# Two attention layers on one core: the second layer's loads issued one by one, ScalarE's exponentials over two or three PSUM banks, and new scheduler weights

## The chip, the cores and the metric

The kernel runs on one core of one Trainium2 chip. The metric is device time in microseconds (us) of one launch; lower is better. Each version was run several times, and a profile was taken of one execution. Engines are named as in the profile: PE (TensorE, matrix multiplications), PEld (its weight loads), DVE (VectorE), ACT (ScalarE), POOL (GpSimd), SP (SyncE, which here only issues DMAs; SPq is its DMA queue). "L757" is line 757 of the kernel's file; the changed kernel has other line numbers for the same code.

## The reference

Two independent layers, A and B, each with 2048 tokens, 512 features and 32 heads of 16 features. A is ordinary softmax attention. B is linear attention with a softmax feature map. The outputs are put side by side.

```python
# A:  q, k, v = split(x @ wqkv)
scores = einsum("bhqd,bhkd->bhqk", q, k) * Dh ** -0.5
o = einsum("bhqk,bhkd->bhqd", softmax(scores), v)          # then  o @ wo
# B:  q, k, v = split(x @ wqkv)
pq, pk = einsum("bhsd,hdf->bhsf", q, w_phi), einsum("bhsd,hdf->bhsf", k, w_phi)
phi_q = concatenate([softmax(pq), softmax(-pq)]);  phi_k = likewise from pk
kv, z = einsum("bhsf,bhsd->bhfd", phi_k, v), sum_s(phi_k)
o = (phi_q @ kv) / (phi_q @ z + 1e-6)                      # then  o @ wo
return concatenate([a, b], axis=-1)
```

A needs 32 x 2048 x 2048, that is 134 million, exponentials. They are what the kernel is about.

## The kernel before

**A program that schedules itself.** The kernel is a Python program. Each piece of work is a `_Task` with an engine, an *assumed* duration `dur`, an assumed latency `lat` until its result can be used, and its dependencies. A greedy list scheduler (`_Sched`) keeps a clock of its own and takes, again and again, the candidate whose start time plus a small priority weight is lowest. It emits the instructions in that order. Each engine's program is that list in that order (below, VectorE waits 11.53 us at one instruction and runs none of those behind it): what the scheduler assumed wrongly can turn into waiting.

```python
sp_q = SC.stream("sp", 0.0)        # DMAs of finished units
sp_b = SC.stream("sp", 0.01)       # B's loads
pe_qd = SC.stream("pe", lambda t: -0.05 if SC.mode == "r" else 0.25)   # weights set by hand
...
c = min(cand, key=lambda c: c[1])  # c[1] = start + weight of its stream
```

**The exponentials.** A's work comes in 32 units (8 groups of four heads x 4 blocks of 512 queries) with 16 key tiles each. One key tile needs four score matmuls (four heads), each filling one PSUM bank of 128 x 512 float32. For about three quarters of the key tiles ScalarE computes the exponentials, two banks per instruction. For the others VectorE makes an approximation by integer arithmetic: four conversions of one bank and three shifted copies. PE then multiplies with V ("PV").

```python
def act_kt(u, kt):
    for half in range(2):
        qk = qk_task(u, kt, half, [("A", A_bank, 1, 1)], lambda t, i: 2 * t.res["A"].idx + i)
        ...
        return e.activation(pT[:, t.res["p"].idx, :], PS[:, b:b + 2, :].rearrange("p a n -> p (a n)"),
                            ACT.Exp, scale=0.25)
        exps.append(put(ac_ex, _Task("act", 0.92, ...)))
```

**The end of a unit.** VectorE copies the finished PSUM bank to `X`, SyncE sends the sums to `sums` by DMA, VectorE takes the reciprocal, SyncE sends it to DRAM (`scr`) and back, spread over the partitions (`Yd`), and GpSimd multiplies. `sums`, `scr` and `Yd` all go through SyncE's queue.

**B's loads** go through the same queue, each list as one task that cannot be split, at an assumed 0.5 us per DMA:

```python
def b_load(name, fn, n, deps, lat, us=0.5):
    d = dsem(name)
    return put(sp_b, _Task("sp", us * n, dma(d, lambda e, t, i: fn(e, i), n), deps, lat=lat))
...
b_wt = b_load("wt", lambda e, i: e.dma_start_transpose(w[...], B_wqkv[...]), 8, freed, 18.0)
b_x  = b_load("xb", lambda e, i: e.dma_start_transpose(xT[:, i, :], B_x[...]), 4, freed, 25.0)
```

Of the kernel before, what the change touches and what calls it, by code (L numbers as in the profile page):

```python
# [124 lines left out]
class _Task:  # L125
    __slots__ = ("eng", "dur", "lat", "deps", "emit", "need", "tok", "end", "res", "then", "rel", "done", "pre",
                 "mode", "rows", "port", "prep", "area", "gate")
# [24 lines left out]
class _Sched:  # L152
# [12 lines left out]
    def __init__(self):  # L165
        self.free = {}
        self.busy = {}
        self.streams = {}
        self.end = 0.0
        self.mode = None  # L170
        self.rows = [0.0] * 4
        self.port = {"dve": 0.0, "pool": 0.0}
        self.urgent = None
        self.last_port = None
        self.filler = None
        self.active = collections.deque()
        self.nfill = 0
        self.nforce = 0
# [8 lines left out]
    @staticmethod  # L187
    def _ready(t):
        r = 0.0
        for d in t.deps:  # L190
            if not d.done:
                return None
            if d.end > r:
                r = d.end
        for _, slots, n, _ in t.need:
            if n == 2:
                fr = [max(x.free, y.free) for x, y in zip(slots, slots[1:]) if x.left == 0 and y.left == 0]
            else:
                fr = [x.free for x in slots if x.left == 0]
            if not fr:  # L200
                return None
            r = max(r, min(fr))
        return r
# [13 lines left out]
    def _choose(self, eng, ss):  # L217
# [17 lines left out]
        if eng == "pe" and self.urgent is not None:  # L235
            u = [c for c in cand if c[2] is self.urgent]
            if u:
                due = max(u[0][3], self.free["act"] - self.MM - self.PE_LAT)
                for c in cand:
                    t = c[2]["q"][0]  # L240
                    if t.mode != "r" and c[0] + t.dur + self.SWITCH > due + 0.02:
                        c[1] += 0.4
# [48 lines left out]
    def _place(self, t, start):  # L291
# [5 lines left out]
        for key, slots, n, nrel in t.need:  # L297
            if n == 2:
                _, _, i = min((max(slots[i].free, slots[i + 1].free) > start, -i, i) for i in range(len(slots) - 1)
                              if slots[i].left == 0 and slots[i + 1].left == 0)  # L300
                got = slots[i:i + 2]
            else:
                got = sorted((x for x in slots if x.left == 0), key=lambda x: (x.free > start, x.idx))[:1]
            for x in got:
                toks += x.take(nrel)
            t.res[key] = got if n > 1 else got[0]
# [29 lines left out]

_LOG2E = 1.4426950408889634
# [6 lines left out]
def _main_path(nc, es, P, dsem, flag, A_x, A_wqkv, A_wo, B_x, B_wqkv, B_w_phi, B_wo, out):  # L344
# [4 lines left out]
    NPT = 7  # L349
    NB, NJ = 2, 4  # L350
    B_AT = (0.24, 0.54, 0.95)
# [53 lines left out]
    pT = sb("pT", [128, NPT, 1024], BF)  # L405
# [9 lines left out]
    A_bank = [_Slot(0), _Slot(1)]  # L415
    G = [_Slot(4), _Slot(5), _Slot(6), _Slot(7)]
# [15 lines left out]
    pe_qa = SC.stream("pe", -0.02)  # L432
    SC.urgent = pe_qa
    pe_tp = SC.stream("pe", -0.15)
    pe_qd = SC.stream("pe", lambda t: -0.05 if SC.mode == "r" else 0.25)
    pe_pj = SC.stream("pe", -0.03)
    pe_pa = SC.stream("pe", left_in(pt_sl, 2, 0.1))
    pe_pd = SC.stream("pe", left_in(rj_sl, 1, 0.1))
    pe_b = SC.stream("pe", 0.02)
    pe_op = SC.stream("pe", -0.03)  # L440
    one_bank = [pe_tp, pe_pj, pe_b, pe_op, pe_pa, pe_pd]
    ac_ev = SC.stream("act", -0.1)
    ac_xe = SC.stream("act", -0.2)
    ac_ex = SC.stream("act", 0.0)
    dv_x = SC.stream("dve", -0.4)
    dv_xe = SC.stream("dve", -0.3)
    dv_ev = SC.stream("dve", -0.2)
    dv_op = SC.stream("dve", -0.2)
    dv_n = SC.stream("dve", -0.15)
    dv_a = SC.stream("dve", -0.1)  # L450
    dv_ad = SC.stream("dve", 0.0)
# [3 lines left out]
    dv_ek = SC.stream("dve", -0.1)  # L455
# [160 lines left out]
    for g in range(1, 4):  # L616
        for c in range(4):
            at.append((32 * (g - 1) + 8 + 4 * c, lambda g=g, c=c: proj("k", g, c)))
        at.append((32 * (g - 1) + 10, lambda g=g: proj("q", g, 0)))
    for i in range(12):  # L620
        at.append((22 + 5 * i, lambda i=i: proj("q", i % 4, 1 + i // 4)))
# [12 lines left out]
    state = {"ua": 0, "ud": 0, "n": 0}  # L634
# [9 lines left out]

    def qk_task(u, kt, half, need, bank):
        g, c = units[u]

        def mm(e, t, i):
            return kq(e, PS[:, bank(t, i), :], u, kt, 2 * half + i)
        return _Task("pe", MM, pe_group(2, mm), [q_ready[(g // 2, c)], k_ready[(g, kt // 4)]], lat=PL, need=need,  # L650
                     mode="r", rows=(2 * half, 2 * half + 1), area=0.5)
# [50 lines left out]
    def make_unit_end(u):  # L702
# [5 lines left out]
        def after_x(_):  # L708
# [15 lines left out]
            for hf in range(2):  # L724
                cs = slice(256 * hf, 256 * hf + 256)
                ms.append(put(po_n, _Task("pool", 0.65, one("pool", lambda e, t, cs=cs: e.tensor_tensor(  # L726
# [20 lines left out]

    def act_kt(u, kt):
        exps = []
        for half in range(2):  # L750
            qk = qk_task(u, kt, half, [("A", A_bank, 1, 1)], lambda t, i: 2 * t.res["A"].idx + i)
            qk_all[u].append(qk)
            put(pe_qa, qk)

            def ex_emit(e, t, qk=qk):
                b = 2 * qk.res["A"].idx
                return e.activation(pT[:, t.res["p"].idx, :], PS[:, b:b + 2, :].rearrange("p a n -> p (a n)"),  # L757
                                    ACT.Exp, scale=0.25)
            exps.append(put(ac_ex, _Task("act", 0.92, one("act", ex_emit), [qk], lat=AL,
                                         need=[("p", pt_sl, 1, 1)], rel=[lambda qk=qk: [qk.res["A"]]])))  # L760
        put(pe_pa, pv_task(u, exps + [v_ready[kt]],
                           lambda h: VP[:, kt, v0(h):v0(h) + 32],
                           lambda r: pT[:, exps[r // 2].res["p"].idx, 512 * (r % 2):512 * (r % 2) + 512],
                           [lambda: [exps[0].res["p"], exps[1].res["p"]]]))
        close(u)

    def dve_kt(u, kt):
        npv[u] += _NPH - 1
        g, c = units[u]
# [35 lines left out]
        for j in range(1, _NPH):  # L805
            ad = put(dv_ad, _Task("dve", 0.59, one("dve", lambda e, t, j=j: e.tensor_scalar(  # L806
                rg[:, t.res["j"].idx, :], rg[:, q0.res["i"].idx, :], float(sh[j]), 32767.0, ALU.add, ALU.min)),
                firsts, lat=DL, need=[("j", rj_sl, 1, 1)], rel=[lambda: [q0.res["i"]]], port=True))
            put(pe_pd, pv_task(u, [ad, vj_ready[(kt, j)]],
# [4 lines left out]
    def src_a(_):  # L814
        while state["ua"] < NU:
            u = state["ua"]
            if a_rem[u]:
                act_kt(u, a_rem[u].pop(0))
                return
            if d_rem[u]:  # L820
                act_kt(u, d_rem[u].pop(0))
                return
            state["ua"] += 1

    def src_d(_):
        u = max(state["ud"], state["ua"])
        while u < NU and (not d_rem[u] or (u == state["ua"] and len(a_rem[u]) + len(d_rem[u]) < 4)):
# [3 lines left out]
        if u > state["ua"] and len(a_rem[u - 1]) + len(d_rem[u - 1]) > 3:  # L831
# [54 lines left out]
    pe_kf, pe_v, pe_kv, pe_qf, pe_y, pe_t, pe_o = (SC.stream("pe", x) for x in (-0.03,) * 7)  # L886
    dv_f, dv_red, dv_v, dv_kv, dv_y, dv_d, dv_ob = (SC.stream("dve", x) for x in (-0.2, -0.1, -0.12, -0.12, -0.12, -0.12, -0.15))
    dv_mn = SC.stream("dve", 0.05)
    ac_kf, ac_qf, ac_ot = (SC.stream("act", x) for x in (-0.1,) * 3)
# [5 lines left out]
    def b_load(name, fn, n, deps, lat, us=0.5):  # L895
        d = dsem(name)
        return put(sp_b, _Task("sp", us * n, dma(d, lambda e, t, i: fn(e, i), n), deps, lat=lat))

    def start_b():
# [4 lines left out]
            B_wqkv[:, (i // 4) * 512 + (i % 4) * 128:(i // 4) * 512 + (i % 4 + 1) * 128]), 8, freed, 18.0)  # L904
        b_x = b_load("xb", lambda e, i: e.dma_start_transpose(  # L905
            xT[:, i, :], B_x[0][:, i * 128:(i + 1) * 128]), 4, freed, 25.0)
# [5 lines left out]
            mask8[:].unsqueeze(1).unsqueeze(3).broadcast_to([128, 4, 8, 16]), ALU.mult)), [b_bd], pre=[t_m8], lat=GL))  # L912
# [3 lines left out]
        def fold(x, ct):  # L916
            f = put(pe_b, _Task("pe", 0.24, pe_group(4, lambda e, t, i: e.matmul(
                PS[:, t.res["b"].idx, i * 128:(i + 1) * 128], w[:, i, x * 512 + ct * 128:x * 512 + (ct + 1) * 128],
                BD[:, i, :], start=True, stop=True)), [b_wt, bd], lat=PL, need=[("b", G, 1, 1)]))
# [11 lines left out]
        def k_step(st):  # L931
# [3 lines left out]
                [b_x] + wf[1], [("b", G, 1, 2), ("e", ek_sl, 1, 2)])  # L935
# [9 lines left out]
            for a in range(2):  # L945
                ph.append(put(po_phi, _Task("pool", 1.0, one("pool", lambda e, t, a=a: e.tensor_tensor(  # L946
# [10 lines left out]
                [b_x, b_wv, bs["vb1"]], [("b", G, 1, 1), ("v", vb_sl, 1, 1)])  # L957
# [35 lines left out]
        def qf_step(cq, t4):  # L993
# [3 lines left out]
                [b_x] + wf[0], [("b", G, 1, 2), ("e", et_sl, 1, 8)])  # L997
            for a in range(2):
                ets[(cq, 2 * t4 + a)] = f, put(ac_qf, _Task("act", 0.49, one("act", lambda e, t, a=a: e.activation(  # L999
                    eT_b[f.res["e"].idx][:, a, :], bank_of(f), ACT.Exp, scale=1.0 - 2.0 * a)),  # L1000
                    [f2] + bs["kend"], lat=AL, rel=[lambda: [f.res["b"]]]))

        def q_step(st):
# [32 lines left out]
            ad = [put(po_y, _Task("pool", 0.65, one("pool", lambda e, t, k=k: e.tensor_tensor(  # L1036
# [8 lines left out]
            for k in range(2):  # L1045
                om.append(put(po_y, _Task("pool", 0.65, one("pool", lambda e, t, k=k: e.tensor_tensor(  # L1046
# [13 lines left out]
                [te, b_wo], [("b", G, 1, 1)])  # L1060
# [40 lines left out]
    c5 = P.op("pe", lambda e: e.matmul(PS[0:1, 4, 0:1], good[:], ones_t[:, 0:1], start=True, stop=True),  # L1101
              [c4] + G[0].toks)
    P.op("dve", lambda e: e.tensor_scalar(flag[0:1, 0:1], PS[0:1, 4, 0:1], 127.5, None, ALU.is_lt), [c5])
# [990 lines left out]
```

## Time and profile before

The time before the change is 829.57 us (median of four runs, 824.21 to 833.1). The profiled span is 829.5 us.

| | before |
|---|---|
| ScalarE busy | 751.4 us (91%) |
| PE busy / VectorE busy | 759.9 us / 736.3 us |
| exponentials on ScalarE | 758, two banks each (1516 banks) |
| mean granted PE clock | 0.959 |

All three large engines are about 90% busy, so shares alone don't tell what bounds the kernel. The page's chain of waits that ended last (share of the span by engine, then by engine and line) does:

```profile
ACT 59%; PE 24%; DVE 11%; SPq 3%; issue 1%; DMA 1%; POOL 0%; ACTq 0%; POOLq 0%
ACT pT L757 55%; PE PS L642 8%; PE PS L657 7%; DVE rg L795 6%; DVE rg L806 3%; PE PS L570 3%; ACT e_k L936 2%; PE PS L567 1%; ACT eT L999 1%; SPq L905 1%; SPq L902 1%; PE PS L1058 1%; PE PS L684 1%; ACT e_k L1055 1%; PE PS L525 1%
```

ScalarE's exponentials (L757) are the backbone, but two fifths of the chain lie elsewhere. The groups view (line, engine, operation, out<-in, count; then busy us, mean ns of one; then idle before it and who ended it) says the same from ScalarE's side:

```profile
L757 ACT ACTIVATE pT<-PS 128x1024 bf16<-128x1024 f32 x758 | 708.6, 1079 | 32.8 <-PE PS L642 28.2
```

**How to count ScalarE's need.** Consecutive instructions overlap, so the mean of 1079 ns is not what one costs. What counts is the distance from one end to the next when nothing is missing. In the trace this is 0.490 us for one bank, 0.917 us for two. Below, *work* is the sum of these distances over all ScalarE operations, and *loss* is the rest of the span. Before: work 743.0 us, loss 86.5 us. Where the loss lies:

| stretch (before) | loss, us |
|---|---|
| 0 to 60 us | 19.7 |
| 60 to 178 us | 6.5 |
| 178 to 232 us | 21.7 |
| 232 us to the last exponential (791.5 us) | 5.0 |
| after the last exponential (less its own work) | 33.6 |

The windows view (stretch, its length, then busy us and count of PE, PEld, DVE, ACT, POOL; then granted PE clock, DMA share, GB/s) shows the first three of these stretches:

```profile
0.00:60.00 60.00, 56.28 (x386) 19.38 (x392) 36.55 (x61) 43.64 (x53) 21.53 (x46) 1.00 0.31 72
60.00:178.00 118.00, 114.69 (x1014) 33.15 (x1028) 110.88 (x190) 110.74 (x120) 13.96 (x20) 0.99 0.05 10
178.00:232.00 54.00, 42.59 (x351) 11.83 (x348) 35.22 (x59) 36.12 (x38) 4.21 (x5) 0.72 0.38 83
```

In the third, every engine slows down at once, and the PE clock falls to 0.72 of full on average. Four timelines (start, length, then the group; in brackets the idle time before it and what ended it) tell why. First SyncE's queue:

```profile
177.36 10.71 SPq L902 DMA_TRANSPOSE w<-in_B_wqkv_dram  x8
188.12 2.48 SPq L733 DMA_DIRECT2D OT<-Oo  x4
190.64 9.43 SPq L905 DMA_TRANSPOSE xT<-in_B_x_dram  x4
200.53 0.41 SPq L907 DMA_DIRECT2D w<-in_B_wqkv_dram  x1
200.99 0.48 SPq L909 DMA_DIRECT2D woB<-in_B_wo_dram  x1
201.53 0.62 SPq L710 DMA_DIRECT2D sums<-X  x1
```

VectorE at the same time:

```profile
190.81 0.68 DVE L704 COPY X<-PS 128x512 f32<-128x512 f32 x1
...
193.81 0.68 DVE L806 TENSOR_SCALAR rg<-rg 128x2048 uint16<-128x2048 uint16 x1
206.02 0.25 DVE L713 RECIPROCAL rin<-sums 128x16 f32<-128x16 f32 x1 [11.53 <-DMA sums<-X]
```

PE, whose next matmul needs what VectorE makes after that reciprocal:

```profile
206.88 0.62 PE L657 MATMUL PS<-rg,VJ 128*32 128x512 f16 x4 [10.74 <-DVE rg L806]
```

And ScalarE:

```profile
178.48 18.51 ACT L757 ACTIVATE pT<-PS 128x1024 bf16<-128x1024 f32 x20 [2.29 <-PE PS L642]
208.07 2.96 ACT L757 ACTIVATE pT<-PS 128x1024 bf16<-128x1024 f32 x3 [11.08 <-PE PS L642]
211.64 1.02 ACT L757 ACTIVATE pT<-PS 128x1024 bf16<-128x1024 f32 x1 [0.60 <-PE PS L642]
213.16 1.02 ACT L757 ACTIVATE pT<-PS 128x1024 bf16<-128x1024 f32 x1 [0.50 <-PE PS L642]
```

`X` is complete at 191.5 us, but its sums leave only at 201.53, after all four transposing loads of B's x. VectorE's reciprocal stands next in order, so VectorE waits 11.53 us; PE waits for VectorE, ScalarE for PE. From about 199 to 230 us PE has half its clock, and ScalarE gets one pair of banks per 1.5 us instead of per 0.92 us. The windows view of that stretch (0.50 is the clock):

```profile
199.00:230.00 31.00, 23.12 (x156) 6.35 (x156) 17.35 (x28) 15.66 (x16) 2.41 (x3) 0.50 0.23 58
```

The scheduler did not see this coming: it assumed 8 x 0.5 = 4 us and 4 x 0.5 = 2 us for lists that took 10.71 and 9.43 us.

### The profile page before, as it was taken

The page shows a single profiled execution, that of the slowest core. Times are in us where ns is not written, and L with a number is a line of the kernel's source. Part 1 is how long each engine was busy: PE and PEld are TensorE (multiplying, and loading weights), DVE is VectorE, ACT ScalarE, POOL GpSimd, SP SyncE. Part 2 cuts the span into 40 slices and gives each one's busy share as a digit, 9 for nine tenths or more (in the row PEclk, how much of TensorE's full clock was granted, in tenths as well). Part 3 has the DMA queues.
Part 4 walks back from the last instruction along what each step waited for, and adds up shares of the span by engine and source line. Part 5 has one row for each costly group of instructions (what it writes and reads, how often), then busy time and mean ns, then how long its engine had stood idle before and what let it go on. Part 6 is the DMA issues. An engine that isn't in the chain of part 4 may idle for free.

```text
span 829.5 us, 17394 instructions
## 1 busy us (share of the span) xinstructions
PE 759.9 (92%) x7165; PEld 231.7 (28%) x7249; DVE 736.3 (89%) x1306; ACT 751.4 (91%) x856; POOL 157.3 (19%) x233
## 2 busy tenths in 40 slices
PE   8999999994999998999989999999999999999963
PEld 3332222221222222222222222223332222332231
DVE  2699999884698999989999999999989999999973
ACT  6879999884699999999999999999999999999930
POOL 5211011110112012221121021005222102302051
PEclk9999999997599999999999999999999999999976
DMA  7100000027000000000000000000000010001001
GB/s 150 54 8 9 11 5 8 8 48 168 7 9 10 14 19 15 12 8 11 10 4 9 27 18 9 12 8 18 15 8 18 14 22 17 20 26 31 9 23 51
DMA packets 44154, 19.61 MB, mean 24 GB/s; under 512 B 33312, under 2 KB 42016, under 8 KB 44064
## 3 DMA queue, kind: packets, MB, share of 16 engines
q1 hardware_dynamic: 42480, 17.60, 8.8%
q8 instruction: 59, 0.97, 0.5%
q10 hardware_dynamic: 1584, 0.79, 0.4%
q14 instruction: 31, 0.25, 0.1%
HBM read 7.88 MB, written 4.46 MB: 15 GB/s over the span
## 4 chain that ended last, share of the span: by engine, by line
ACT 59%; PE 24%; DVE 11%; SPq 3%; issue 1%; DMA 1%; POOL 0%; ACTq 0%; POOLq 0%
ACT pT L757 55%; PE PS L642 8%; PE PS L657 7%; DVE rg L795 6%; DVE rg L806 3%; PE PS L570 3%; ACT e_k L936 2%; PE PS L567 1%; ACT eT L999 1%; SPq L905 1%; SPq L902 1%; PE PS L1058 1%; PE PS L684 1%; ACT e_k L1055 1%; PE PS L525 1%
## 5 line engine op out<-in xcount | busy, mean ns | idle before, releaser
L757 ACT ACTIVATE pT<-PS 128x1024 bf16<-128x1024 f32 x758 | 708.6, 1079 | 32.8 <-PE PS L642 28.2
L642 PE MATMUL PS<-QT,KT 32*128 32x512 bf16 x2048 | 352.0, 389 | 21.7 <-ACT pT L757 13.1
L795 DVE TENSOR_SCALAR rg<-PS 128x512 uint16<-128x512 f32 x532 | 340.5, 680 | 18.1 <-PE PS L642 16.1
L806 DVE TENSOR_SCALAR rg<-rg 128x2048 uint16<-128x2048 uint16 x399 | 260.6, 693 | 4.6 <-PE PS L657 4.1
L642 PEld LDWEIGHTS PS<-QT,KT 32*128 32x128 bf16 x2048 | 89.5, 91 | 302.4 <-ACT pT L757 218.0
L657 PE MATMUL PS<-rg,VJ 128*32 128x512 f16 x1596 | 147.9, 389 | 11.0 <-DVE rg L806 10.7
L657 PE MATMUL PS<-pT,VP 128*32 128x512 bf16 x1516 | 151.7, 397 | 2.2 <-ACT pT L757 1.1
L657 PEld LDWEIGHTS PS<-pT,VP 128*32 128x32 bf16 x1516 | 38.3, 94 | 87.4 <-issue 65.8
L726 POOL TENSOR_TENSOR OT<-X,Yd 128x256 bf16<-128x256 f32 x32 | 22.7, 727 | 198.4 <-DVE rg L806 155.3
L946 POOL TENSOR_TENSOR w<-e_k,stat 128x512 bf16<-128x512 bf16 x32 | 33.2, 1056 | 136.1 <-DVE rmin L952 42.6
L657 PEld LDWEIGHTS PS<-rg,VJ 128*32 128x32 bf16 x1596 | 39.0, 95 | 68.4 <-issue 31.5
L657 PE MATMUL PS<-rg,VP 128*32 128x512 f16 x532 | 53.2, 390 | 0.0
L726 POOL TENSOR_TENSOR Oo<-X,Yd 128x256 bf16<-128x256 f32 x32 | 23.1, 738 | 108.1 <-DMA Yd<-scr 55.2
L1036 POOL TENSOR_TENSOR w<-w 128x272 f32<-128x272 f32 x32 | 23.8, 760 | 98.5 <-DVE w L1022 80.3
L570 PE MATMUL PS<-xT,w 128*128 128x512 bf16 x111 | 30.6, 383 | 3.5 <-issue 1.9
L1055 ACT ACTIVATE e_k<-PS 128x512 bf16<-128x512 bf16 x16 | 10.1, 631 | 20.8 <-PE PS L1052 20.8
L684 PE MATMUL PS<-ones_t,zer 128*32 128x512 bf16 x276 | 28.4, 409 | 0.0
L704 DVE COPY X<-PS 128x512 f32<-128x512 f32 x32 | 22.0, 686 | 4.8 <-PE PS L657 3.6
L1022 DVE TENSOR_TENSOR w<-PS,stat 128x408 f32<-128x408 f32 (+1 forms) x48 | 25.2, 526 | 0.6
L1046 POOL TENSOR_TENSOR w<-w,den 128x256 bf16<-128x256 f32 x32 | 19.8, 636 | 31.3 <-DVE rg L806 9.3
L1058 PE MATMUL PS<-woB,e_k 128*128 128x512 bf16 x50 | 17.5, 435 | 4.6 <-issue 1.8
L939 DVE TENSOR_REDUCE stat<-e_k 128x64 f32<-128x1024 bf16 x16 | 19.3, 1209 | 0.1
(85 smaller groups left out, 422.8 us busy)
## 6 DMA issues: line engine op xcount, KB each, us to landing
Yd<-scr SPq DMA_DIRECT2D x128, 32.0 KB, 1.8
out_dram<-OA SPq DMA_DIRECT2D x16, 128.0 KB, 1.7
out_dram<-e_k SPq DMA_DIRECT2D x16, 128.0 KB, 1.7
OT<-Oo SPq DMA_DIRECT2D x64, 16.0 KB, 1.8
w<-in_A_wqkv_dram SPq DMA_DIRECT2D x2, 384.0 KB, 4.9
OT<-in_A_x_dram SPq DMA_DIRECT2D x1, 512.0 KB, 4.6
w<-in_A_wqkv_dram ACTq DMA_DIRECT2D x1, 512.0 KB, 7.7
WOp<-in_A_wo_dram SPq DMA_DIRECT2D x1, 512.0 KB, 6.8
```

The costliest lines, as they stand in the source:

```text
L570: return e.matmul(bank_of(t), w[:, ct, c0:c0 + 128], xT[:, ct, c * 512:(c + 1) * 512], start=(ct == 0), stop=(ct == 3))
L642: return e.matmul(out_ap, KT[32 * r:32 * r + n, g, kt * 128:(kt + 1) * 128], QT[32 * r:32 * r + n, c, g // 2, :], start=True, stop=True, t ...
L657: return e.matmul(PS[32 * r:32 * r + 32, pvb[u].idx, :], lhs(8 * (g // 2) + 2 * r + g % 2), rhs(r), start=t.res["first"], stop=t.res["last ...
L684: P.op("pe", lambda e, r=r: e.matmul(PS[32 * r:32 * r + 32, pvb[u].idx, :], zer[:], ones_t[:].unsqueeze(1).broadcast_to([128, 4, 128]), st ...
L726: ms.append(put(po_n, _Task("pool", 0.65, one("pool", lambda e, t, cs=cs: e.tensor_tensor(OT[:, c % 2, g // 2, cs] if even else Oo[:, ms[0 ...
L757: return e.activation(pT[:, t.res["p"].idx, :], PS[:, b:b + 2, :].rearrange("p a n -> p (a n)"), ACT.Exp, scale=0.25)
L795: return e.tensor_scalar(rg[:, q0.res["i"].idx, 512 * r:512 * r + 512], PS[:, qk.res["D"].idx, :], ya, yb, ALU.mult, ALU.add)
L806: ad = put(dv_ad, _Task("dve", 0.59, one("dve", lambda e, t, j=j: e.tensor_scalar(rg[:, t.res["j"].idx, :], rg[:, q0.res["i"].idx, :], flo ...
L946: ph.append(put(po_phi, _Task("pool", 1.0, one("pool", lambda e, t, a=a: e.tensor_tensor(pk[ph[0].res["k"].idx][:, 512 * a:512 * a + 512]. ...
L1022: muls.append(put(dv_y, _Task("dve", 0.485, one("dve", lambda e, t, yv=yv, lo=lo, n=n: e.tensor_tensor(ysv[r0.res["y"].idx][:, 136 * lo:13 ...
L1036: ad = [put(po_y, _Task("pool", 0.65, one("pool", lambda e, t, k=k: e.tensor_tensor(y3(0)[:, 2 * k:2 * k + 2], y3(0)[:, 2 * k:2 * k + 2], ...
L1058: o1, o2 = two_step(pe_o, lambda e, t, i: e.matmul(bank_of(t), oT_b[tp.res["t"].idx][:, i, :], woB[:, i, :], start=(i == 0), stop=(i == 3) ...
```

## The change

Its intent is to stop B's loads from blocking the finished units' DMAs, and to let ScalarE take three banks at once where a bank beside the pair is free. The scheduler's priority weights were also drawn anew (all now in one table `_W`), and the buffer of exponentials holds 15 single banks instead of 7 pairs. The core of the diff, with cuts marked:

```diff
     def b_load(name, fn, n, deps, lat, us=0.5):
         d = dsem(name)
-        return put(sp_b, _Task("sp", us * n, dma(d, lambda e, t, i: fn(e, i), n), deps, lat=lat))
+        return [put(sp_b, _Task("sp", us, dma(d, lambda e, t, r, i=i: fn(e, i)), deps, lat=lat)) for i in range(n)]
 ...
-            B_wqkv[...]), 8, freed, 18.0)
+            B_wqkv[...]), 8, freed, 4.0, 1.32)
-            xT[:, i, :], B_x[0][:, i * 128:(i + 1) * 128]), 4, freed, 25.0)
+            xT[:, i, :], B_x[0][:, i * 128:(i + 1) * 128]), 4, freed, 8.0, 2.5)
 ...   # PSUM: pairs at banks 0-1 and 3-4, single bank 2 beside both
-    A_bank = [_Slot(0), _Slot(1)]
-    G = [_Slot(4), _Slot(5), _Slot(6), _Slot(7)]
+    A_bank = [_Slot(0), _Slot(3)]
+    G = [_Slot(5), _Slot(6), _Slot(7), _Slot(2)]
 ...   # score matmuls are now taken from a list `pend`, two or three at a time
+            if len(pend) > 2 and x.left == 0 and x.free <= max(own.free, SC.free["pe"]) + 0.02 and \
+                    sum(y.left == 0 for y in G) > _W["el"]:
+                n = 3
 ...
+        us = 0.187 + 0.3657 * n            # the assumed duration of an exponential over n banks
+            return e.activation(pT[:, p:p + n, :].rearrange("p a n -> p (a n)"),
+                                PS[:, b:b + n, :].rearrange("p a n -> p (a n)"), ACT.Exp, scale=0.25)
 ...   # the guard that keeps long PE work from delaying score matmuls
-                due = max(u[0][3], self.free["act"] - self.MM - self.PE_LAT)
+                due = max(u[0][3], self.free["act"] + self.ahead() - self.MM - self.PE_LAT - _W["early"])
-                        c[1] += 0.4
+                        c[1] += _W["guard"]        # 0.346
 ...   # all weights and positions, e.g.
-    pe_tp = SC.stream("pe", -0.15)
-    pe_qd = SC.stream("pe", lambda t: -0.05 if SC.mode == "r" else 0.25)
+    pe_tp = SC.stream("pe", _W["tp"])                                              # -0.276
+    pe_qd = SC.stream("pe", lambda t: _W["qd_r"] if SC.mode == "r" else _W["qd_o"])  # 0.115, 0.235
-    B_AT = (0.24, 0.54, 0.95)          # when B's phases start
+    B_AT = (_W["b0"], _W["b1"], _W["b2"])                                          # 0.315, 0.54, 0.99
```

## The prediction

> **What bounds the kernel now.** The chain of waits that ended last is 59% ScalarE, 55% of it the exponentials over two PSUM banks. The groups view gives 758 of them, 1079 ns each; in the chain they follow each other every 0.917 us (22 in 20.18 us). Single-bank ScalarE operations follow every 0.49 us (two in 0.98). So ScalarE needs about 758 x 0.917 + some 97 smaller operations = 742 us; the other 85-88 us of the 829.5 us span are time in which it starved. By windows (length minus operations times cadence):
> - 0-60 us: 20 us lost (loads, projections);
> - 120-178: 7.6 us;
> - 197-232: 18.5 us;
> - 232-791: about 3 us in all, ScalarE is saturated;
> - after 791: 35 us, the serial tail.
>
> The loss at 197-232 is one event. The timeline of the SyncE queue shows 8 transposing loads of B's weights (10.7 us), 4 copies, then 4 transposing loads of B's x (9.4 us), each list one indivisible step. The sums of a finished unit, whose X copy ended at 191.4 us, are sent only at 201.5 us; VectorE's reciprocal waits 11.5 us for them and holds up everything behind it in order. ScalarE idles 197-208, and PE's granted clock then is 0.5 until about 230 us, when ScalarE gets one pair per 1.5 us. The Trainium skill ("TensorE: Matmul & The Clock Gate", Part 1) says that idleness halves the clock; the trace agrees (0.50 in 200-220).
>
> **What the change does.**
> 1. B's loads become single steps. In the new order on the SyncE queue the sums go out after the 8th weight transpose, before x's loads, the rest between x's transposes. I expect a wait of 1-3 us instead of 11.5 and no lowered clock: 14-17 us saved, all critical.
> 2. Exponentials: 629 over two banks, 91 over three, one over one. A cadence line through 0.49 and 0.917 gives 1.34 us for three (slope 0.427 us per 512 columns; the Trainium skill, "ScalarE: Activation LUTs", "What ACT_TABLE_LOAD costs", states 0.833 ns per element, which agrees). Estimate: a third bank saves only 0.03 us per three-bank operation, 3 us in all; the kernel's own model hopes for 1.28 us. But ScalarE takes 16 banks more (1532 against 1516): +7 us. Net +4 us on ScalarE.
> 3. VectorE loses 16 conversions and 12 adds: 16 x 0.60 + 12 x 0.60 = 17 us less. PE switches its mode less often and gets 57 more filler groups. Neither bounds 232-791, so this mostly becomes slack; it may take 2-4 us off the losses before 178 us.
> 4. B's steps move later: six final output steps after the last exponential, not five, at about 5 us each; the last two are back to back and A's last output chain overlaps. Tail 0-3 us longer.
>
> **Sum.** 830 - 16 + 4 - 3 + 1 - (scattered gaps, other new weights) 4 = 812 us.
>
> **What would show it.** No ScalarE gap over 3 us around B's loads, and clock near 1.0 there; reciprocal's wait for sums under 3 us; three-bank cadence 1.34 (not 1.28); VectorE busy near 720; ScalarE's need about 746; tail 35-39 us after the last exponential.
>
> **What would make it wrong.** Smaller DMAs that queue behind x's transposes land late and stall VectorE anew; triples take the bank that other work needs and starve PE; a longer tail because B's steps crowd the end; or the retuned priorities remove more of the start's 20 us than I think. Runs of before span 824 to 833, so the 2% verdict is close to a coin toss.
>
> I predict 812 us, 799 to 824 in 8 of 10 cases; faster by over 2%: 0.52, within 2%: 0.45, slower: 0.03.

## More of the kernel before

A gap counts in the stretch in which the operation behind it starts. So the gap of 2.29 us that ends at 178.48 us stands in the third stretch, although it comes behind nine projection matmuls on PE at 175.00 us and not from the loads.

The early loss has another look. PE at 45 to 51 us:

```profile
45.16 2.20 PE L567 MATMUL PS<-w,xT 128*128 128x512 bf16 x9 [0.16 <-issue]
47.19 3.62 PE L570 MATMUL PS<-xT,w 128*128 128x512 bf16 x16
50.73 0.61 PE L657 MATMUL PS<-pT,VP 128*32 128x512 bf16 x8
```

and ScalarE beside it:

```profile
46.52 0.60 ACT L578 ACTIVATE VP<-PS 128x512 bf16<-128x512 f32 x1 [1.97 <-PE PS L567]
51.19 15.81 ACT L757 ACTIVATE pT<-PS 128x1024 bf16<-128x1024 f32 x17 [4.06 <-PE PS L657]
```

Twenty-five projection matmuls run in a row without a score matmul (L642) or a PV between them, and ScalarE runs dry for 4 us.

## The result and the profile after

The changed kernel takes **798.31 us** (median of four runs, 794.7 to 801.79), against 829.57 us for the kernel before. The ratio is 0.9628, with a 95% interval from 0.9554 to 0.9702: faster by more than 2%. Ratios here and below are the mean time of one kernel's fast runs over that of the other's fast runs of the same rounds, so they are not quite the ratio of the medians quoted. The predicted range ended at 799 us, so the measured time lies just outside it, on the fast side, 14 us below the predicted figure.

| | before | after |
|---|---|---|
| profiled span | 829.5 us | 798.9 us |
| ScalarE work | 743.0 us | 747.5 us |
| loss, 0 to 60 us | 19.7 | 11.4 |
| loss, 60 to 178 us | 6.5 | 0.1 |
| loss, 178 to 232 us | 21.7 | 0.0 |
| loss, 232 us to the last exponential | 5.0 | 6.2 |
| loss after the last exponential | 33.6 | 33.5 |
| VectorE busy | 736.3 us | 721.9 us |
| mean granted PE clock | 0.959 | 0.981 |

B's loads run from 147 to 174 us in the changed kernel, so the stretch to set beside 178 to 232 us of before is 140 to 194 us. The windows view after:

```profile
0.00:60.00 60.00, 56.38 (x388) 18.32 (x396) 35.83 (x60) 51.06 (x60) 22.34 (x47) 1.00 0.33 73
60.00:178.00 118.00, 113.70 (x1108) 32.13 (x1121) 112.00 (x193) 118.00 (x122) 16.12 (x22) 1.00 0.20 44
140.00:194.00 54.00, 51.85 (x559) 15.49 (x556) 52.93 (x92) 54.00 (x56) 7.63 (x10) 1.00 0.41 89
```

ScalarE is busy for all 54.00 us around the loads, at full PE clock. SyncE's queue there:

```profile
160.65 0.61 SPq L714 DMA_DIRECT2D sums<-X  x1
161.30 5.05 SPq L974 DMA_TRANSPOSE xT<-in_B_x_dram  x2
166.40 0.58 SPq L720 DMA_DIRECT2D scr<-rin  x1
```

The sums leave before x's transposes, and VectorE's reciprocal has no wait before it:

```profile
163.35 0.24 DVE L717 RECIPROCAL rin<-sums 128x16 f32<-128x16 f32 x1
```

ScalarE is fed without a gap from 38.73 us on (the row names one shape, but holds all exponentials of the stretch, the three-bank ones too):

```profile
38.73 205.30 ACT L795 ACTIVATE pT<-PS 128x1024 bf16<-128x1024 f32 x210
```

PE at the place where the kernel before had its burst of projections (here L581; L654 are the score matmuls):

```profile
46.97 0.39 PE L654 MATMUL PS<-QT,KT 32*128 32x512 bf16 x2
47.29 0.60 PE L581 MATMUL PS<-xT,w 128*128 128x512 bf16 x2
47.83 0.39 PE L654 MATMUL PS<-QT,KT 32*128 32x512 bf16 x2
48.15 0.60 PE L581 MATMUL PS<-xT,w 128*128 128x512 bf16 x2
```

Two projections, then two scores, and so on: each step is short enough for ScalarE not to run dry. The chain of waits after (L795 are the exponentials):

```profile
ACT 83%; PE 12%; DVE 3%; issue 1%; POOL 0%; ACTq 0%; POOLq 0%
ACT pT L795 78%; PE PS L654 3%; PE PS L661 3%; ACT e_k L1005 2%; PE PS L581 1%; ACT eT L1068 1%; PE PS L1127 1%; DVE rg L852 1%; PE PS L536 1%; ACT e_k L1124 1%; DVE rg L873 1%; PE PS L578 1%; PE PS L918 1%; ACT Wf L1068 0%; ACT VP L589 0%
```

And the exponentials in the groups view, kept apart by shape:

```profile
L795 ACT ACTIVATE pT<-PS 128x1024 bf16<-128x1024 f32 x629 | 600.9, 1097 | 4.5 <-PE PS L654 4.3
L795 ACT ACTIVATE pT<-PS 128x1536 bf16<-128x1536 f32 x91 | 138.1, 1518 | 0.0
```

The idle time before them fell from 32.8 to 4.5 us. A three-bank one ends 1.344 us after the operation before it (median of 91), the value predicted from the line through one and two banks, 0.063 + 0.427 us per bank.

### The profile page after: what moved, and what is told of

Its sections match the earlier page's. It is cut to its first block, busy times and chain, and to the rows that moved or that the text cites. A ratio compares the mean times of both kernels' runs of the same rounds, so it can differ in the third digit from the quotient of the medians.

```text
span 798.9 us, 17735 instructions
## 1 busy us (share of the span) xinstructions
PE 730.0 (91%) x7368; PEld 221.6 (28%) x7429; DVE 721.9 (90%) x1278; ACT 752.3 (94%) x819; POOL 157.4 (20%) x233
## 4 chain that ended last, share of the span: by engine, by line
ACT 83%; PE 12%; DVE 3%; issue 1%; POOL 0%; ACTq 0%; POOLq 0%
ACT pT L795 78%; PE PS L654 3%; PE PS L661 3%; ACT e_k L1005 2%; PE PS L581 1%; ACT eT L1068 1%; PE PS L1127 1%; DVE rg L852 1%; PE PS L536 1%; ACT e_k L1124 1%; DVE rg L873 1%; PE PS L578 1%; PE PS L918 1%; ACT Wf L1068 0%; ACT VP L589 0%
## 5 line engine op out<-in xcount | busy, mean ns | idle before, releaser
L795 ACT ACTIVATE pT<-PS 128x1024 bf16<-128x1024 f32 (+2 forms) x721 | 708.5, 1149 | 4.5 <-PE PS L654 4.3
L852 DVE TENSOR_SCALAR rg<-PS 128x512 uint16<-128x512 f32 x516 | 331.8, 681 | 17.9 <-PE PS L654 15.4
L654 PE MATMUL PS<-QT,KT 32*128 32x512 bf16 x2048 | 308.2, 387 | 32.0 <-ACT pT L795 26.8
L873 DVE TENSOR_SCALAR rg<-rg 128x2048 uint16<-128x2048 uint16 x387 | 251.2, 690 | 3.5 <-PE PS L661 3.0
L654 PEld LDWEIGHTS PS<-QT,KT 32*128 32x128 bf16 x2048 | 78.5, 91 | 292.1 <-ACT pT L795 230.4
L661 PE MATMUL PS<-rg,VJ 128*32 128x512 f16 x1548 | 142.7, 388 | 0.4
L661 PE MATMUL PS<-rg,VP 128*32 128x512 f16 x516 | 50.8, 384 | 0.2 <-DVE rg L852 0.2
L688 PE MATMUL PS<-ones_t,zer 128*32 128x512 bf16 x504 | 47.2, 388 | 0.0
L581 PE MATMUL PS<-xT,w 128*128 128x512 bf16 x114 | 34.0, 382 | 3.0 <-issue 1.9
L1124 ACT ACTIVATE e_k<-PS 128x512 bf16<-128x512 bf16 x16 | 10.3, 641 | 20.4 <-PE PS L1121 20.3
L1115 POOL TENSOR_TENSOR w<-w,den 128x256 bf16<-128x256 f32 x32 | 19.4, 623 | 27.9 <-PE PS L1121 12.4
L1008 DVE TENSOR_REDUCE stat<-e_k 128x64 f32<-128x1024 bf16 x16 | 19.4, 1215 | 0.7 <-ACT e_k L1005 0.4
```

The lines of the kernel that those rows point to most:

```text
L581: return e.matmul(bank_of(t), w[:, ct, c0:c0 + 128], xT[:, ct, c * 512:(c + 1) * 512], start=(ct == 0), stop=(ct == 3))
L654: return e.matmul(out_ap, KT[32 * r:32 * r + n, g, kt * 128:(kt + 1) * 128], QT[32 * r:32 * r + n, c, g // 2, :], start=True, stop=True, t ...
L661: return e.matmul(PS[32 * r:32 * r + 32, pvb[u].idx, :], lhs(8 * (g // 2) + 2 * r + g % 2), rhs(r), start=t.res["first"], stop=t.res["last ...
L688: P.op("pe", lambda e, r=r: e.matmul(PS[32 * r:32 * r + 32, pvb[u].idx, :], zer[:], ones_t[:].unsqueeze(1).broadcast_to([128, 4, 128]), st ...
L795: return e.activation(pT[:, p:p + n, :].rearrange("p a n -> p (a n)"), PS[:, b:b + n, :].rearrange("p a n -> p (a n)"), ACT.Exp, scale=0.25)
L852: return e.tensor_scalar(rg[:, q0.res["i"].idx, 512 * r:512 * r + 512], PS[:, qk.res["D"].idx, :], ya, yb, ALU.mult, ALU.add)
```

## The experiments

The question was where the 31 us come from: from the loads, from the exponentials' new form, or from the new weights. Fourteen runs were made, one of them of the changed kernel again; all were correct and had three or five rounds beside runs of the kernel before on the same chip. "Loss" and "work" are as above, from the profiled execution. The theories were:

- *The stall is the gain.* B's loads cost about 15 to 20 us; undoing their part brings these back, doing it alone brings them in.
- *The new exponentials are the gain*, by the third bank or by the guard that knows the queue of exponentials (`SC.ahead`).
- *The weights are the gain*, since they decide how work is interleaved.
- *The draw.* Any edit makes the greedy scheduler draw another order for everything after it, and that alone moves the time by several us; then no single edit can be read by itself.

### First call: one part at a time

**Loads alone.** The kernel before, with the load lines of the diff (durations and latencies too) and nothing else.

```diff
-        return put(sp_b, _Task("sp", us * n, dma(d, lambda e, t, i: fn(e, i), n), deps, lat=lat))
+        return [put(sp_b, _Task("sp", us, dma(d, lambda e, t, r, i=i: fn(e, i)), deps, lat=lat)) for i in range(n)]
 ... (the durations and latencies of the two lists, and their uses)
```

> Kernel before with one part of the change: B's loads as single steps with the measured durations (1.32 and 2.5 us each). Theory A (the list of loads cost 21-22 us of ScalarE's time at 178-232 us; the early losses come from old priorities): that stage's loss falls from 21.5 to under 5 us, the 25 us lost before 178 us stay, span 808-815 us, ratio 0.975-0.98. Rival B (three-bank exponentials with finer buffers give the runway that hides the loads): the stage keeps over 10 us of loss, ratio above 0.985.

Measured: 831.42 us (829.56 to 833.3), ratio 1.007 [1.0, 1.014]: no gain at all. Yet the stall is gone: the loss in 178 to 232 us fell from 21.7 to 3.3 us. It came back elsewhere. The loss between 232 us and the last exponential rose from 5.0 to 12.0 us, and the loss after it from 33.6 to 53.1 us; ScalarE's work fell by 7.3 us (1500 banks instead of 1516), so this is another draw. ScalarE's timeline at the end shows the largest piece:

```profile
777.23 0.60 ACT L1055 ACTIVATE e_k<-PS 128x512 bf16<-128x512 bf16 x1 [2.91 <-PE PS L1052]
790.57 1.08 ACT L999 ACTIVATE eT<-PS 128x512 bf16<-128x512 f32 x2 [12.74 <-PE PS L995]
```

A step of B's queries is left to the very end. This is a different order of everything, not a price of the loads; but at this point that was only a guess.

**Lists again.** The changed kernel with the two loads as indivisible lists and their old assumed durations and latencies.

```diff
-        return [put(sp_b, _Task("sp", us, dma(d, lambda e, t, r, i=i: fn(e, i)), deps, lat=lat)) for i in range(n)]
+        return [put(sp_b, _Task("sp", us * n, dma(d, lambda e, t, i: fn(e, i), n), deps, lat=lat))]
 ... (the durations and latencies of the two lists as before)
```

> Changed kernel with B's loads put back into two indivisible lists with the old assumed durations. Theory A: the stall comes back, 15-22 us of ScalarE time lost around the loads and a clock near 0.5 there, span 815-822. Rival B: under 8 us slower than the changed kernel.

Measured: 828.2 us (824.3 to 830.58), ratio 1.0017 [0.9945, 1.0088]: the whole gain is lost. The stall is back; ScalarE's timeline:

```profile
159.46 5.23 ACT L795 ACTIVATE pT<-PS 128x1024 bf16<-128x1024 f32 x5
177.46 1.02 ACT L795 ACTIVATE pT<-PS 128x1024 bf16<-128x1024 f32 x1 [12.77 <-PE PS L654]
```

But the loss grew by 22 us in all (51.4 to 73.8), of it 14 around the loads, and ScalarE's work grew by 7.5 us (1548 banks instead of 1532), so here too the schedule was drawn anew. The two runs contradict each other if each is read as "the price of the loads": 0 us one way, 30 us the other.

**No third bank.**

```diff
-          p0=8, p1=22, p2=5.753, lone=0, psh=0, pn=4, ps=-0.308, el=2, both=0)
+          p0=8, p1=22, p2=5.753, lone=0, psh=0, pn=4, ps=-0.308, el=9, both=0)
```

> Changed kernel without third banks: every exponential over two banks, new priorities and single loads kept. Theory A (a third bank saves 0.03 us per three-bank operation, 91 of them): work of ScalarE 2-3 us more, losses before 178 us stay near 11 us, span 799-805. Rival B (the third bank is what removed the early losses and gave 13 us): losses before 178 us grow by 8 us or more, span above 808.

Measured: 797.44 us (797.37 to 802.44), ratio 0.968 [0.9608, 0.9751]. The changed kernel itself has 798.31 us and 0.9628. So a schedule without the third bank, one of the things the change is named after, is as fast. What the bank itself is worth this does not show: ScalarE's work grew by 4.7 us (1536 banks) and the loss fell by 7.9 us, so here too the schedule was drawn anew.

**The old weights.** The changed kernel with the streams' weights of before; the positions of B's steps stay new.

```diff
-_W = dict(tp=-0.276, qa=-0.02, qd_r=0.115, qd_o=0.235, pj=-0.051, pa_n=3, pa_w=0.053, pd_n=0, ...
+_W = dict(tp=-0.15, qa=-0.02, qd_r=-0.05, qd_o=0.25, pj=-0.03, pa_n=2, pa_w=0.1, pd_n=1, ...
```

> Changed kernel with the priorities of before (weights of the streams, guard, lead), but the new positions of B's steps, three-bank exponentials and single loads. Theory A (retuned priorities spread the projections and removed 13 us of loss before 178 us): those losses come back, 8-14 us, span 806-815. Rival B (three banks did it): within 4 us of the changed kernel.

Measured: 808.75 us (806.37 to 812.58), ratio 0.9812 [0.9742, 0.9882]. Half of the gain stays. The loss of the first eighth of the exponentials is 14.9 us, against 20.1 before and 11.5 after, and after the last exponential it is 39.9 us. The guard and `lead`, which bounds how early VectorE starts on the next unit, went back too, as the expectation says; ScalarE's work was 6.4 us less (1516 banks).

### Second call: combinations, and the durations

**Loads and A's weights, old exponentials.** The loads-alone kernel with the new weights of A's streams and the guard at 0.346.

```diff
-    pe_qd = SC.stream("pe", lambda t: -0.05 if SC.mode == "r" else 0.25)
+    pe_qd = SC.stream("pe", lambda t: 0.115 if SC.mode == "r" else 0.235)
 ... (15 more such lines, the guard's among them)
```

> Kernel before with single-step loads (as e1_singles) plus the changed priorities of A's streams alone; two-bank exponentials as before, B's priorities and positions as before. e1_singles removed 20 us of loss at the loads and gave 19.5 us back in the tail (53 us after the last exponential, against 34). Theory A2 (single loads free the time, retuned priorities keep B's last steps out of the tail): tail back to 32-40 us, no loss over 8 us at the loads, span 802-814. Rival B2 (finer exponential buffers and the new code are needed for the gain): span above 820.

Measured: 815.12 us (806.69 to 816.69, five runs), ratio 0.9868 [0.9806, 0.993]. The loss in the first 60 us is 15.8 us, from 20.8 in the loads-alone kernel, and the tail is normal again (32.7 us).

**Without the look ahead.** The changed kernel without one line.

```diff
-    SC.ahead = lambda: state["qk"]
```

> Changed kernel whose PE guard no longer counts the exponentials that are queued for ScalarE (as before the change). If the guard is what spread the projections, the losses of the first quarter of the exponentials rise from 11.6 us to 20 or more and the span to 810 or more. If not, the first quarter stays under 15 us; the rest of the schedule shifts by some us, span 798-808.

Measured: fast runs of 809.11, 817.99 and 819.31 us; ratio 0.9865 [0.9772, 0.9957]. The profiled run was slow, so its trace is not used, and where those 17 us or so lie stays open.

**Lists with the right durations.** As "lists again", but with the measured durations and latencies for the tasks (8 x 1.32 us, 4 x 2.5 us).

```diff
-        return [put(sp_b, _Task("sp", us, dma(d, lambda e, t, r, i=i: fn(e, i)), deps, lat=lat)) for i in range(n)]
+        return [put(sp_b, _Task("sp", us * n, dma(d, lambda e, t, i: fn(e, i), n), deps, lat=lat))]
```

> Changed kernel with B's loads in two indivisible lists, as in e2_lists, but with the measured durations (10.6 and 10 us) in the scheduler. Theory A3 (the scheduler's wrong durations, not the indivisibility, made the stall: with the right ones the sums go out between the lists): loss at the loads under 4 us, span 798-812. Rival B3 (indivisible lists stall whatever durations are assumed): 8 us or more lost at the loads, span above 815.

Measured: 811.34 us (807.93 to 815.42), ratio 0.9831 [0.9763, 0.99]. The lists are indivisible as before, and still there is no stall. SyncE's queue and then ScalarE, around the loads:

```profile
158.75 2.17 SPq L723 DMA_DIRECT2D Yd<-scr  x4
160.96 0.61 SPq L714 DMA_DIRECT2D sums<-X  x1
161.62 9.18 SPq L974 DMA_TRANSPOSE xT<-in_B_x_dram  x4
```

```profile
139.60 61.01 ACT L795 ACTIVATE pT<-PS 128x1024 bf16<-128x1024 f32 x61
```

So an indivisible list need not make the stall. In this draw a scheduler that knows that the list holds the queue for 9 us sent the sums first by itself. The run changed the assumed latencies together with the durations and drew the schedule anew, so which of the two matters is not shown; that the order on the queue decides is shown in the fifth call. The kernel is slower than the changed one because ScalarE has 16 banks more to do (work 755.2 against 747.5 us, with the same loss: 51.0 against 51.4 us). That again is the draw.

### Third call: how much is the draw?

Two controls change nothing of substance: every weight of the changed kernel moves by 0.003 up or down, at random.

```diff
-_W = dict(tp=-0.276, qa=-0.02, qd_r=0.115, qd_o=0.235, pj=-0.051, pa_n=3, pa_w=0.053, pd_n=0, pd_w=0.055,
+_W = dict(tp=-0.273, qa=-0.017, qd_r=0.118, qd_o=0.238, pj=-0.054, pa_n=3, pa_w=0.05, pd_n=0, pd_w=0.052, ...
```

> Control: the changed kernel with every priority weight moved by 0.003 up or down at random, nothing else. Theory C (the greedy schedule is chaotic and the retuned weights are a lucky draw, so that undoing any part costs some 10 us whatever that part does): span 808-822, with no loss at B's loads and the loss spread over other stages. Rival (the weights matter by their sense, not their digits): within 4 us of the changed kernel's 798.

Measured: 814.12 us (812.07 to 817.51), ratio 0.9847 [0.9782, 0.9911].

> A second such control, with other random signs; the scheduler's own estimate of its span is 6 us above that of the changed kernel, against 21 us for nudge12. Theory C: span 800-812, between the changed kernel and nudge12, no loss at B's loads. Rival: within 4 us of 798, as nudge12.

Measured, with other signs: 801.76 us (800.3 to 804.78), ratio 0.9708 [0.965, 0.9767].

An edit without meaning can cost 16 us. In the first control the early loss is back (18.5 us in the first eighth, 11.5 in the changed kernel), and 8.6 us more are lost in the fourth eighth. So the changed kernel is a lucky draw, or a searched one (two controls can't tell; the scheduler's own clock had put them 21 and 6 us above the changed kernel, the measured differences are 16 and 3 us), and experiments that redraw the schedule can't settle parts of 10 us. What was needed was an experiment that leaves all other orders as they are.

### Fourth call: does a search do better?

The assumed duration of an exponential was set to the measured line, and the weights were searched again on the scheduler's own clock; once with the third bank, once without. The changed kernel ran beside them.

```diff
-        us = 0.187 + 0.3657 * n
+        us = 0.063 + 0.427 * n
 ... (and other values in _W)
```

> Changed kernel with the measured cost of an exponential in the scheduler (0.063 + 0.427 us per bank, so 1.344 us for three banks instead of the assumed 1.284) and the weights searched anew with it. If the schedule is a lottery in which a search on true costs draws better: span 785-797. If a search on the scheduler's own clock does not carry over to the chip: 798 or more. No loss at B's loads in either case.

> The same search without third banks (two banks per exponential). If the third bank is worth only the 0.03 us per operation that its cadence shows: within 5 us of e10_tuned, span 787-800, and at or below the changed kernel. If the third bank matters as a buffer: 8 us or more above e10_tuned.

> The changed kernel unaltered, on the same chip as the two above: 794-802, as recorded; it gives the width of its own spread, 3 to 8 us between executions.

| kernel | median us (range, runs) | ratio to before [95%] |
|---|---|---|
| searched anew, three banks allowed | 795.31 (792.79 to 797.01, 6) | 0.9599 [0.9558, 0.9639] |
| searched anew, pairs only | 804.13 (799.17 to 806.48, 6) | 0.9691 [0.9645, 0.9736] |
| the changed kernel, unaltered | 800.62 (797.13 to 801.9, 6) | 0.9659 [0.9618, 0.9699] |

The first is the fastest version. All six of its runs are below all six of the changed kernel, by 5 us in the medians, though the intervals of the two ratios still overlap a little. The pairs-only search gave a worse draw than simply switching the third bank off in the changed kernel did (797.44 us), so this pair of runs says nothing about the third bank.

### Fifth call: the orders fixed

Here the schedule is made as always, and afterwards only the twelve entries of SyncE's queue around x's loads are put in another order. All other engines keep their lists, instruction for instruction.

In the kernel before, the sums go ahead of x's transposes, and the rest of that unit's DMAs between them:

```diff
+    q = P.streams["sp"].items
+    i = next(n for n, x in enumerate(q) if x[2] == "xb")
+    x, b, u = q[i:i + 4], q[i + 4:i + 6], q[i + 6:i + 12]
 ... (an assertion that these are the entries meant)
+    q[i:i + 12] = u[:1] + x[:2] + u[1:2] + x[2:3] + u[2:] + x[3:] + b
```

> Kernel before with the order of twelve entries of the SyncE queue alone changed, after all scheduling: the sums of the finished unit go out before B's x loads, its other small copies between them, as in the changed kernel. All other engines keep their order instruction by instruction. Theory D (the late sums cost ScalarE about 20 us, and e1_singles gave that back only because its whole schedule was drawn anew): no wait over 3 us for the sums, loss of the second eighth 27.5 to 6-10 us, tail unchanged at 33-35 us, span 806-813. Rival D2 (the time is given back later whatever the order, because something else bounds the rest): span above 820.

In the changed kernel, the reverse: x's four transposes and B's two plain loads first, then the unit's DMAs.

```diff
+    q = P.streams["sp"].items
+    i = next(n for n, x in enumerate(q) if x[2] == "xb") - 1
+    seg = q[i:i + 12]
+    x = [k for k in seg if k[2] in ("xb", "wv", "wob")]
+    u = [k for k in seg if k not in x]
 ... (the same assertion)
+    q[i:i + 12] = x + u
```

> The reverse: changed kernel with the sums and the copies behind B's x loads, everything else in its order. Theory D: 14-22 us lost at the loads, half clock there, tail and other stages as in the changed kernel, span 812-822. Rival D2: under 6 us slower than the changed kernel.

Measured: the first takes 812.59 us (809.16 to 817.66), ratio 0.9792 [0.9712, 0.9872]; the second 816.03 us (813.6 to 820.25), ratio 0.9851 [0.9778, 0.9924]. Forward, the stall alone is worth 17 us (829.61 us for the kernel before, less 812.59; the interval of the ratio allows 11 to 24 us). Backward it costs 15 to 18 us (816.03 less 800.62 or 798.31; the profiled spans differ by 13.3 us).

The windows and timelines show that it is the same stall. The kernel before with SyncE's queue reordered, 178 to 232 us:

```profile
178.00:232.00 54.00, 52.20 (x540) 16.14 (x532) 52.80 (x88) 54.00 (x62) 8.99 (x11) 1.00 0.43 86
```

The changed kernel with the queue put back, SyncE and then ScalarE:

```profile
160.33 9.37 SPq L974 DMA_TRANSPOSE xT<-in_B_x_dram  x4
169.74 1.15 SPq L976 DMA_DIRECT2D w<-in_B_wqkv_dram  x1
170.93 0.51 SPq L978 DMA_DIRECT2D woB<-in_B_wo_dram  x1
171.48 0.61 SPq L714 DMA_DIRECT2D sums<-X  x1
```

```profile
139.37 25.40 ACT L795 ACTIVATE pT<-PS 128x1024 bf16<-128x1024 f32 x27
178.42 1.45 ACT L795 ACTIVATE pT<-PS 128x1536 bf16<-128x1536 f32 x1 [13.65 <-PE PS L654]
```

The loss in 178 to 232 us goes from 21.7 to 0.1 us in the first; in the second, 18.5 us appear around its loads, where there was none. In the first, 2.3 of these 21.6 us are not the stall: the gap behind the nine projections is still there, but ends at 177.56 us and so counts one stretch earlier. Of the 19.3 us of the stall, 3.3 us are lost again after 232 us (5.0 to 8.3), and the span falls by 16.5 us. In the second, about 5 us are won back after 232 us. The two runs agree with each other, and together with the result they leave 12 to 16 us of the gain to everything else: the kernel before with the stall taken away has 812.59 us, the changed kernel 798 to 801 us; and the changed kernel with the stall put in is still 12 us faster than the kernel before (the ratio of 0.9851).

## Why the prediction was right or wrong

The prediction was 812 us in a range from 799 to 824; the measured median is 798.31 us. "Faster by over 2%", called the likeliest at 0.52, is what came. Term by term, in us of the profiled spans:

| term of the sum | predicted | measured by the loss account | measured with orders fixed |
|---|---|---|---|
| the stall at B's loads | -16 | -19.4 | -17 and, in reverse, +15 to +18 |
| ScalarE's work | +4 | +4.5 | |
| losses before 178 us, scattered gaps, new weights | -3 and -4 | -17.0 (before 178 us), +1.2 (after 232 us) | |
| tail | +1 | -0.1 | |
| sum | -18 | -30.8 | |

(The sum differs from the difference of the spans, 30.6 us, by rounding. The gap of 2.29 us behind the nine projections is counted here before 178 us, not with the stall: 21.7 less 2.3, and 26.2 plus 2.3 less 11.5.)

**Right: the mechanism of the stall.** The sums go out before x's loads; ScalarE has no gap and the clock is 1.00 there. With all other orders fixed the stall is worth 17 us (11 to 24), about the predicted 14 to 17. The Trainium skill ("TensorE: Matmul & The Clock Gate", Part 1) says that idleness halves PE's clock. The trace agrees as to the halving: PE idled from 196.1 to 206.9 us, and the clock fell to 0.50 at 199.1 us, 3 us into this. "All critical" was right only with the orders fixed. In the loads-alone kernel, whose schedule was drawn anew, the gain was given back in full, most of it in the tail.

**Right: ScalarE's work.** The three-bank distance is 1.344 us, as predicted, not the 1.284 us that the kernel's scheduler assumes. The Trainium skill ("ScalarE: Activation LUTs", "What ACT_TABLE_LOAD costs") gives 0.833 ns per element; the trace's slope of 0.427 us per 512 elements agrees. Since the time per element is the same in long instructions, a third bank saves only fixed parts: an estimate from the line is 0.063 us times one half per three-bank operation, 3 us for 91 of them. No run could tell these 3 us from nothing.

**Wrong: the size of the early losses.** The step that failed is item 3 of the prediction, "this mostly becomes slack; it may take 2-4 us off the losses before 178 us", together with the "4" for "scattered gaps, other new weights". The losses before 178 us fell by 17.0 us, from 28.5 to 11.5. They were read correctly from the profile before, as sizes (20 us by 60 us, more after 120). The mistake was to count only 2 to 4 us of them, and another 4 for scattered gaps, as removable. About 11 us stay in the changed kernel, in the kernel without the third bank, in the second control and in both searched kernels (10.3 to 11.5 us in the first eighth). The rest were waits behind runs of projections on PE. In the trace before, ScalarE waits more than 1 us seven times between 20 and 179 us, 14.7 us in all (at 26, 36, 46, 51, 122, 163 and 178 us), each time at or just behind a run of 9 to 25 projections in a row (25 at 45 us, 14 at 160, 9 at 175); in the trace after, no wait between 12.2 and 240 us is longer than 0.5 us. The kernel before with SyncE's queue reordered keeps the seven waits, and the first control, where the early loss is back, has 38 projections in a row at 22.6 us. So the traces show where the time was lost and won; no run changed PE's order alone, and which part of the change broke up the runs stays open. The prediction named this case among what would make it wrong ("the retuned priorities remove more of the start's 20 us than I think") and did not price it. It could have been priced: the order of PE's instructions in the new kernel was known before any run, and there, at the place of the 25, they come in twos.

**Wrong, and of little effect: the account of the stall itself.** The prediction subtracted a remaining wait of 1 to 3 us for the reciprocal. There was none, and the loss at the loads fell to 0.0 us.

**Near right: the tail.** Six final steps instead of five were expected to cost 0 to 3 us; the loss after the last exponential is 33.6 and 33.5 us, and from there to the end it is 38.0 and 38.4 us, within the predicted 35 to 39. The last two steps were issued back to back, as foreseen.

**What stays open.** How the other 12 to 16 us divide between the look ahead, the weights and the exponentials' finer grain. Each single edit redraws the schedule, and the controls show that a redraw alone moves the time by up to 16 us. The removal of the look ahead cost about 17 us in its fast runs, and the return to the old weights about 10 us; neither is clearly more than the draw can do.

## What to carry to other kernels

When a static scheduler orders a kernel, its assumed durations are part of the program: a DMA list taken for 2 us held its queue for 9 us, and the order that came of it cost 17 us; with the right durations and latencies the scheduler avoided it in one draw even with the list undivided. Don't judge one part of such a change by undoing it and letting the scheduler draw again; first run a control with a meaningless nudge, and then change only the order under dispute after scheduling. When pricing a new schedule, look for starved stretches in the old one, subtract what every version has to pay at the start, and read from the new instruction order whether the rest can still happen.

## What the Trainium skill lacked or had wrong

- "DMA: Bandwidth & Descriptors", "Issuing engines are not separate DMA queues", says that the sequencer's time to initiate a DMA "is usually small relative to the DMA itself". For the transposing loads here it is not. A load of one weight block held SyncE's queue for 1.26 us (median of 8), while the data landed 2.7 us after issue; a load of 128 columns of x held it for 2.36 us (median of 4), landing after 4.8 us. The page gives no issue time on trn2 for a transposing DMA of this size, and it was these 9.43 us on the queue that the sums waited behind.
- "ScalarE: Activation LUTs", "What ACT_TABLE_LOAD costs", gives 186 ns + 0.833 ns per element for one instruction with immediate operands and an overlap of about 93 ns. That makes 1039 ns for 1024 elements and 1466 ns for 1536. An isolated pair in the stall took 1.02 us, which agrees; in a full queue the profile shows means of 1079 and 1097 ns (before and after) and of 1518 ns for three banks, so a mean of busy time overstates the cost. The distance between ends is 0.490, 0.917 and 1.344 us, against 0.520, 0.946 and 1.373 us by the page's numbers: the same slope, and about 29 ns less. The page does not say whether reading across two or three PSUM banks costs anything; at 0.427 us per bank it does not.
- "TensorE: Matmul & The Clock Gate", Part 1, lets the clock recover after about one busy window of 3.4 us. Here PE was busy without a break from 206.9 us on, and the clock stayed at 0.50 until 229.8 us, 22.9 us later (16.6 us in the changed kernel with the queue put back). Nor was every halving behind an idle window of that length: in the changed kernel the clock was 0.50 from 419.8 to 430.1 us, though PE had not idled for more than 0.2 us at a time in the 7 us before. The page does not say how busy such a window must be when the matmuls use only part of the array, as the score and PV matmuls do here.
- No page speaks of how far a greedy schedule's time moves under edits without meaning: 16 us of 800 here, for weights moved by 0.003.
